# RWKV attention into a GELU layer: the pairs of zero products behind the first tile's bursts are left out

## The chip, the cores and the metric

One core of one Trainium2 chip runs the whole program. The time is the device's, in microseconds (us), from launch to end; the kernel before was run three times: 587.01, 589.43 and 590.76 us, median 589.43. Engines: TensorE (PE; its weight loads are listed apart as PEld), VectorE (DVE), ScalarE (ACT), GpSimd (POOL) and SyncE (SP), which issues most of the transfers.

## What is computed

For each of 4 batches and 8 heads (head size 48, 768 time steps) a state of 48 x 48 is carried through time. Its rows decay by `w`, and each step adds an outer product:

```
cur   = (u * k_t) outer v_t
y_t   = r_t @ (state + cur)
state = w_t[:, None] * state + k_t outer v_t
```

The y of all heads, laid side by side, are 3072 rows of 384 columns. They go through a layer: h = x @ w_in (384 x 2048), the exact GELU, and @ w_out (2048 x 384). All inputs are float32 or are turned into it in the kernel.

## The kernel before

The time axis is cut into tiles of 384 steps, two per batch: eight tiles, numbered x = 0 to 7. While the layer of tile x - 1 runs, the attention of a later tile is prepared beside it. The order of the work is written by hand: each tile has a string in `PLAN`, in which every letter takes one step of one generator ("." and "s" are the two units of tile 0, "f" the next tile's attention, "c" the conversion of the weights, "l" the loads, "x" larger groups of zero products). Engines then work through their own queues in that order and wait for one another by semaphores.

Inside a tile, steps are handled in chunks of 64. Within a chunk the matrix of decayed products r·k is built by halves: for each level h = 1, 2, 4, 8, 16, 32 (`LEVELS`, `halves()`), TensorE multiplies k by r for all chunks (a burst), the blocks of that level are copied out of PSUM into `a_sb`, and VectorE multiplies the decay over h steps into r and k, so that the next level can use them. So the next burst of a unit waits for that unit's update, and an update waits for the burst before it, which still reads r and k.

Tile 0 is special. It starts before any layer work is there, and its heads are split into two units that alternate, so that one unit's burst can run beside the other's update. Level 1 of a unit is done in `with_diagonal()` (L497); levels 2 to 32 in `products()` (burst at L478). Results go into pairs of PSUM banks from a pool of three (`pair`). Updates are at L557 (levels 2 to 16) and L546 (level 1, the k of level 32); copies into `a_sb` at L506, L508 and L570 on VectorE, and for levels 16 and 32 at L565 on ScalarE. After the levels come the transposes of k (L744, copied out at L746), the products k·v (L791) and a·v (L781), the chain of states on VectorE (L806), a fence (L822), the products of r with the state (L855), the copies to x transposed (L862, L878, L885), and then the layer's first product h (L1282). The weights arrive as 64-bit floats and are converted piece by piece on ScalarE (L356 to L359) and VectorE (L368, L372).

The kernel also issues products whose operands are zeros and whose result nobody reads (`keep_warm`, L248): each is a 128 x 128 load and a 512-wide bfloat16 product into a PSUM bank. 14 stand at the start, 7 behind the first unit's level 1 and 7 behind the products a·v of tile 0 (`warm()`), and in tile 0 two behind every burst of `products()`: 48 in all, 20 of them behind bursts. Those behind bursts use a single bank from `bank()`, which takes the two single banks in turn.

Of the kernel before, what the change touches and what calls it, by code (L numbers as in the profile page):

```python
# [91 lines left out]
def kernel(  # L92
# [31 lines left out]
    def pair(name):  # L124
        return pools["d"].tile([128, 2, BANK], F32, name=name, tag="d")
# [14 lines left out]
    def bank(name="o_ps"):  # L140
        turns[0] ^= 1
        return ps.tile([128, BANK], F32, name=name, tag=f"mm{turns[0]}")
# [99 lines left out]
    def keep_warm(n, elsewhere=False):  # L242
        if elsewhere:
            t = pair("warm")[:, 0]
        else:
            t = bank("warm")
        for _ in range(n):
            nc.tensor.matmul(t, lhsT=zeros[:, 0:128], rhs=zeros, start=True, stop=True)  # L248
# [127 lines left out]
    def attention(x, unit):  # L376
# [91 lines left out]
        else:  # L468
            yield

        def products(bs, right, width, rest=False):
            d = pair("d")
            n = 0
            for b in bs:
                for i in range(NI):
                    for g in range(2):
                        for p in range(2):
                            nc.tensor.matmul(d[half[p], g, n * width:(n + 1) * width],  # L478
                                             lhsT=kc[half[g], b, i, p], rhs=right(half[g], b, i, p),
                                             start=True, stop=True)  # L480
                    n += 1
            if x == 0 and not rest:
                keep_warm(2)
            return d[:, :, 0:n * width]

        def with_diagonal():
# [24 lines left out]
        def diagonal():  # L511
            return [products([b], lambda z, b, i, p: rucs[b][z, i, p], C) for b in range(np_)]
# [7 lines left out]
        def halves():  # L520

            for h in LEVELS:
                m = C // 2 // h
                if np_ < NPART and h == 1:
                    ds = with_diagonal()
                elif np_ < NPART:
                    d = products(range(np_), lambda z, b, i, p: rc[z, b, i, p], C)
                    d = d.rearrange("p g (n m two j) -> p g n m two j", two=2, j=h, m=m)[:, :, :, :, 1, :]
                else:
                    right = rc.rearrange("p b i c (m two j) -> p b i c m two j", two=2, j=h)[:, :, :, :, :, 1, :]  # L530
                    d = products(range(np_), lambda z, b, i, p: right[z, b, i, p], C // 2)
                    d = d.rearrange("p g (n m j) -> p g n m j", j=h, m=m)
# [1003 lines left out]
```

## Time and profile before

| | |
|---|---|
| median of three runs | 589.43 us |
| profiled execution | 587.12 us, span 585.3 us |
| TensorE busy | 567.1 us, 97% of the span |
| weight loads busy | 506.5 us, 87% |
| VectorE busy | 466.3 us, 80% |
| ScalarE busy | 307.4 us, 53% |
| zero products (L248) | 48, 14.5 us busy, 2.3 to 38.3 us |
| first product of the layer, h (L1282) | starts at 44.24 us |
| first product with w_out (L1371) | starts at 90.69 us |

The profile is one execution with every instruction's start and duration. A row of the timeline gives the start, the length, the engine, the line, what it writes and reads, the shape, and the number of instructions merged; in square brackets stands how long the engine was idle before, and which event ended that. A float32 product appears as two records (24 products of a burst are x48). The records of a product overlap, since products are pipelined: a single record's duration is longer than the time from one start to the next.

### The profile page before, as it was taken

How to read it: one execution, taken by the hardware profiler on the slowest of the kernel's cores; microseconds unless marked ns; L12 is line 12 of the kernel's file. 1: busy time of each engine (PE TensorE's matmuls, PEld its weight loads, DVE VectorE, ACT ScalarE, POOL GpSimd, SP SyncE). 2: the span in 40 equal slices, each digit the busy share in tenths (PEclk: the TensorE clock that was granted, in tenths of full speed). 3: DMA queues.
4: the chain of work that ended last, by engine and by line, in shares of the span. 5: the costliest groups of instructions: out<-in, count | busy, mean ns of one | idle time of the engine just before them, and what ended most of it. 6: DMA issues, size and time to landing. Idle time of an engine off the chain costs nothing.

```text
span 585.3 us, 17572 instructions
## 1 busy us (share of the span) xinstructions
PE 567.1 (97%) x7494; PEld 506.5 (87%) x7494; DVE 466.3 (80%) x914; ACT 307.4 (53%) x731; POOL 9.4 (2%) x29
## 2 busy tenths in 40 slices
PE   7799999999999999999998999999999999999997
PEld 3576666699998899999998899999999999999997
DVE  6889958999979998687978999577988999543523
ACT  2568997236363465545563457535654357425510
POOL 3200000000000000000000000000000000000000
PEclk9999999999999999999999999999999999999999
DMA  8449931111032311430124210430114100210000
GB/s 303 173 123 357 369 129 46 34 62 54 3 78 79 101 49 19 100 119 11 46 39 127 86 38 6 110 111 31 55 23 131 44 3 2 42 46 1 1 16 33
DMA packets 51006, 46.82 MB, mean 80 GB/s; under 512 B 31728, under 2 KB 36080, under 8 KB 50928
## 3 DMA queue, kind: packets, MB, share of 16 engines
q1 hardware_dynamic: 50160, 45.11, 24.9%
q8 instruction: 59, 0.97, 0.7%
q10 hardware_dynamic: 768, 0.59, 0.4%
q14 instruction: 19, 0.16, 0.1%
HBM read 36.24 MB, written 4.72 MB: 70 GB/s over the span
## 4 chain that ended last, share of the span: by engine, by line
PE 53%; DVE 5%; DMA 1%; issue 0%; ACT 0%; DVEq 0%; ACTq 0%
PE o_ps L1156 23%; PE u_ps L1032 16%; PE h_ps L1032 7%; PE d L654 3%; PE y_ps L781 1%; PE y_ps L855 1%; DMA out_dram<-o_sb 1%; PE kv_ps L791 1%; DVE e L1130 1%; DVE st L806 1%; DVE f L1130 1%; PE d L646 0%; DVE s L1130 0%; DVE tot_sb L437 0%; DVE o_sb L1130 0%
## 5 line engine op out<-in xcount | busy, mean ns | idle before, releaser
L1032 PE MATMUL u_ps<-x_home,w_in_sb 128*128 128x192 f32 x364 | 69.4, 329 | 0.5 <-DVE g L1069 0.4
L1032 PEld LDWEIGHTS u_ps<-x_home,w_in_sb 128*128 128x128 f32 x364 | 60.0, 190 | 2.3 <-DVE g L1069 1.1
L1156 PE MATMUL o_ps<-w_out_sb,g 128*128 128x192 f32 x224 | 41.0, 331 | 0.0
L1043 ACT ACTIVATE g<-g 128x384 f32<-128x384 f32 x66 | 32.5, 520 | 10.1 <-DVE g L1069 10.1
L1156 PEld LDWEIGHTS o_ps<-w_out_sb,g 128*128 128x128 f32 x224 | 36.4, 190 | 1.3
L670 ACT COPY a_sb<-d 32x256 f32<-32x256 f32 (+8 forms) x90 | 32.6, 363 | 8.5 <-PE d L654 7.0
L1072 ACT COPY g<-u_ps 128x384 f32<-128x384 f32 x56 | 26.6, 480 | 19.8 <-PE u_ps L1032 18.6
L1069 DVE TENSOR_TENSOR g<-g,h_ps 128x384 f32<-128x384 f32 x42 | 23.0, 548 | 14.8 <-PE h_ps L1032 14.8
L1282 PE MATMUL h_ps<-xT,w_in_sb 128*128 128x384 f32 x96 | 33.7, 497 | 0.7 <-ACT rkw L1287 0.6
L1165 ACT COPY o_sb<-o_ps 128x192 f32<-128x192 f32 x29 | 9.3, 319 | 47.2 <-PE o_ps L1156 38.0
L1156 PE MATMUL o_ps<-w_out_sb,f 128*128 128x192 f32 x176 | 30.9, 328 | 1.6 <-ACT o_sb L1165 1.6
L1156 PE MATMUL o_ps<-t,e 128*128 128x192 f32 x176 | 31.7, 331 | 0.0
L806 DVE SCALAR_TENSOR_TENSOR st<-st,tot,kv_ps 128x48 f32<-128x48 f32 x120 | 21.9, 258 | 12.2 <-PE kv_ps L791 12.2
L1156 PE MATMUL o_ps<-t,s 128*128 128x192 f32 x176 | 31.2, 330 | 0.0
L1156 PE MATMUL o_ps<-w_out_sb,e 128*128 128x192 f32 x176 | 30.9, 327 | 0.0
L1156 PEld LDWEIGHTS o_ps<-w_out_sb,f 128*128 128x128 f32 x176 | 28.8, 190 | 2.0 <-ACT o_sb L1165 1.9
L1156 PE MATMUL o_ps<-t,g 128*128 128x192 f32 x176 | 30.4, 326 | 0.0
L1156 PEld LDWEIGHTS o_ps<-t,e 128*128 128x128 f32 x176 | 28.6, 190 | 1.0 <-ACT o_ps L1172 0.3
L1032 PE MATMUL h_ps<-xT,w_in_sb 128*128 128x192 f32 x140 | 28.2, 332 | 1.1 <-issue 1.1
L1069 DVE TENSOR_TENSOR g<-g,u_ps 128x384 f32<-128x384 f32 x42 | 22.8, 550 | 7.8 <-PE u_ps L1032 7.5
L1156 PEld LDWEIGHTS o_ps<-w_out_sb,e 128*128 128x128 f32 x176 | 28.8, 190 | 0.1
L1156 PEld LDWEIGHTS o_ps<-t,s 128*128 128x128 f32 x176 | 28.6, 190 | 0.4
(215 smaller groups left out, 1266.2 us busy)
## 6 DMA issues: line engine op xcount, KB each, us to landing
rkw<-in_rkw_dram SPq DMA_DIRECT2D x54, 256.0 KB, 3.4
raw<-in_w_out_dram SPq DMA_DIRECT2D x8, 768.0 KB, 7.1
v_in<-in_v_dram SPq DMA_DIRECT2D x8, 584.0 KB, 4.6
raw<-in_w_in_dram SPq DMA_DIRECT2D x5, 768.0 KB, 6.6
out_dram<-o_sb SPq DMA_DIRECT2D x20, 192.0 KB, 2.0
kt_home<-x_home SPq DMA_DIRECT2D x72, 48.0 KB, 2.1
rkw<-in_rkw_dram SPq DMA_DIRECT2D x6, 384.0 KB, 5.9
raw<-in_w_in_dram SPq DMA_DIRECT2D x9, 256.0 KB, 5.3
```

Source lines behind the costliest of these rows:

```text
L654: nc.tensor.matmul(o[half[p], i * 3 * C // 2:(i + 1) * 3 * C // 2], lhsT=kc[half[g], n // NI, n % NI, p], rhs=rx[half[g], 2 * n + p], star ...
L670: nc.scalar.copy(out=at[z, g, first:behind, (a + 1) * h:], in_=d[z, :, :, to] if g == slice(None) else d[z, :, to])
L781: nc.tensor.matmul(y[p][half[g ^ swap(b)], i * C:(i + 1) * C], lhsT=vs(b, i, g)[half[p]], rhs=at[half[p], g, b * NI + i, :], start=(i == 0 ...
L806: nc.vector.scalar_tensor_tensor(out=stq[:, q, c], in0=stq[:, q, c - 1] if c else b4[:, q, NC - 1], scalar=totq[:, q, c:c + 1], in1=kvs[q ...
L1032: nc.tensor.matmul(o, lhsT=lhsT, rhs=rhs, start=start, stop=True, skip_group_check=True)
L1043: nc.scalar.activation(out=o, in_=z, func=AF.Gelu, scale=scale)
L1069: nc.vector.tensor_add(o, *(a if len(a) > 1 else (o, a[0])))
L1072: nc.scalar.copy(out=o, in_=a)
L1130: steps.append(("a", lambda: f(*(a() for a in args))))
L1156: nc.tensor.matmul(t[name], lhsT=lhs(j), rhs=rhs(j), start=start and j == 0, stop=(j == HF - 1), skip_group_check=True)
L1165: return lambda: nc.scalar.copy(out=to(), in_=t[name])
L1282: nc.tensor.matmul(h_ps, lhsT=w_in_sb[:, f // FI, j, f % FI * 128:(f % FI + 1) * 128], rhs=xT[:, j, :], start=(j == 0), stop=(j == NJ - 1))
```

## The change

`products()` no longer issues two zero products behind its burst in tile 0; its argument `rest`, which no caller sets, goes with it. The 28 other zero products stay.

```
-        def products(bs, right, width, rest=False):
+        def products(bs, right, width):
             d = pair("d")
             n = 0
             for b in bs:
...
                     n += 1
-            if x == 0 and not rest:
-                keep_warm(2)
             return d[:, :, 0:n * width]
```

More of the change, by code (lines that the diff above doesn't have):

```diff
@@ L469, in attention, with products @@
             yield
-        def products(bs, right, width, rest=False):
+        def products(bs, right, width):
             d = pair("d")
@@ L481, in products @@
                     n += 1
-            if x == 0 and not rest:
-                keep_warm(2)
             return d[:, :, 0:n * width]
```

## The prediction

> **What bounds the kernel now.** I read the page's busy shares and chain first, then the waits, then the timelines of TensorE (PE), VectorE (DVE) and ScalarE (ACT) from 8 to 48 us, where the removed products stand.
>
> ```profile
> PE 567.1 (97%) x7494; PEld 506.5 (87%) x7494; DVE 466.3 (80%) x914; ACT 307.4 (53%) x731; POOL 9.4 (2%) x29
> ...
> PE 53%; DVE 5%; DMA 1%; issue 0%; ACT 0%; DVEq 0%; ACTq 0%
> ...
> 50.00:55.00 5.00, 5.00 (x108) 3.35 (x107) 4.90 (x9) 4.97 (x9) 0.00 (x0) 1.00 1.05 392
> 55.00:60.00 5.00, 5.00 (x108) 3.35 (x107) 5.00 (x6) 4.81 (x7) 0.00 (x0) 1.00 1.05 398
> ```
>
> PE is the bound overall; from 44 us on it has hardly a gap (two lines of the table by stretch are shown: span, PE, PE loads, DVE, ACT busy, then clock and DMA). So a microsecond by which that dense part starts earlier is a microsecond at the end, if nothing between takes it back. The removed products lie earlier, between 12.7 and 31.8 us. PE's rows there (start, duration, what):
>
> ```profile
> 12.67 0.61 PE L248 MATMUL warm<-zeros 128*128 128x512 bf16 x2
> 14.02 0.93 PE L478 MATMUL d<-rkw 64*64 64x64 f32 x48 [0.74 <-DVE rkw L557]
> 14.88 0.60 PE L248 MATMUL warm<-zeros 128*128 128x512 bf16 x2
> 15.41 1.54 PE L497 MATMUL d<-rkw 64*64 64x128 f32 x48
> ...
> 18.99 0.61 PE L248 MATMUL warm<-zeros 128*128 128x512 bf16 x2
> 19.64 0.93 PE L478 MATMUL d<-rkw 64*64 64x64 f32 x48
> ...
> 24.72 0.93 PE L478 MATMUL d<-rkw 64*64 64x64 f32 x48 [1.05 <-DVE rkw L557]
> 25.58 0.60 PE L248 MATMUL warm<-zeros 128*128 128x512 bf16 x2
> 26.11 0.93 PE L478 MATMUL d<-rkw 64*64 64x64 f32 x48
> ```
>
> And DVE's rows that had to wait for such a burst:
>
> ```profile
> 20.63 1.84 DVE L557 TENSOR_TENSOR rkw<-rkw,tot_sb 128x768 f32<-128x768 f32 x2 [0.22 <-PE d L478]
> ...
> 28.51 0.96 DVE L557 TENSOR_TENSOR rkw<-rkw,tot_sb 128x768 f32<-128x768 f32 x1 [0.44 <-PE d L478]
> ...
> 29.91 0.56 DVE L546 TENSOR_TENSOR rkw<-rkw,tot_sb 128x384 f32<-128x384 f32 x1 [0.41 <-PE d L478]
> 31.30 0.56 DVE L546 TENSOR_TENSOR rkw<-rkw,tot_sb 128x384 f32<-128x384 f32 x1 [0.84 <-PE d L478]
> ```
>
> To see: up to 25 us PE waits for DVE (idle 0.74 and 1.05 us before bursts), and most pairs of zeros fill such idle time. From 25.6 to 31.6 it turns: burst, zeros, burst, zeros without a gap, and DVE waits.
>
> **The change, part by part.** It removes ten pairs of zero products (20 loads, 20 products) and adds nothing. The instruction lists agree otherwise, on every engine. Ten turns of the two single PSUM banks go too; ten is even, so later users get the same bank. A pair costs PE 0.53 us: 25.58 to 26.11. All ten: 5.3 us. What counts is what they hold up. I call the units A and B with their level, in PE's order: A2, A4, B1, A8, B2, B4, B8, A16, B16, A32, B32.
>
> 1. Behind A2 (12.67): nothing. A4 waits for DVE until 14.02.
> 2. Behind A4 (14.88): B1 can start at 14.90 instead of 15.41 and end at 16.44. DVE's update after B1 started at 17.11, B1's end (16.95) plus 0.16; DVE was free at 16.47. So it starts at 16.60: 0.51 earlier. (The profile calls that 0.64 us of DVE idle "issue", but it ends with the burst.)
> 3. Behind A8 (18.99): A8 stands still until 18.14 after four of its products, marked "issue"; I leave that moment where it is, so A8 ends at 19.0. B2 then follows at once, ends near 19.9, and DVE's update at 20.63 can start at 20.0 (DVE is free at 19.9): 0.6 earlier in all.
> 4. Behind B2 and B4 (20.50, 23.07): nothing of their own; B4 and B8 wait for DVE, which is busy 4.78 of the 5 us from 20 to 25. The 0.6 stays.
> 5. Behind B8 (25.58): A16 runs at 25.0 to 25.9, but DVE reaches A16's update only at 27.45, after B8's masked copy: still about 0.6.
> 6. Behind A16 (26.98): B16 starts at 26.1 after B8's update, ends at 27.0. DVE, free at 27.45, updates it then instead of 28.51: 1.06 earlier.
> 7. Behind B16: A32 needs A16's update (27.45): 27.5 to 28.4, its update 28.5 instead of 29.91: 1.4.
> 8. Behind A32: B32 at 28.45 to 29.4, its update 29.45 instead of 31.30: 1.85.
> 9. Behind B32 (31.17): the transposes, 31.61 before, can run at 29.55. They need PSUM that ACT's ten copies (L565, 27.16 to 30.86) release, and these start when B8's masked copy ends, 0.6 earlier. The copies end at 30.25, so ACT's copy of the first transpose, 32.46 before, starts at 30.35: 2.1.
>
> What is late next is thus ACT's row of copies, not DVE or PE. Behind it stands a chain without slack: k·v products (33.31), ten state updates a unit (34.66 and 36.70), the fence (38.46), the products with the state (38.66), x transposed, h at 44.24; each waits for the one before, so 2.1 passes on. I take **2.0**, of ends 0 and 2.1 while the clock holds. 0 would be a fixed time behind: from 48 to 75 us ACT is nearly full too (4.97 and 4.81 of 5) and the DMA share is 1.05. I choose near 2.1 because the weights' transfers that fill that stretch are issued from 43.21 on, behind this same chain, and move with it; and the last piece of w_in is converted at 66 to 67 us and first read at 84.21.
>
> Against the profiled execution, 587.12 us (span 585.3): 585.1. That execution was 2.3 below the median of 589.43; against the median, **587.4**.
>
> **The clock: the other half of the change.** The page prints a granted clock of 1.0 everywhere, but the records of the zeros themselves show two speeds:
>
> ```profile
> L248 PE MATMUL warm<-zeros x8: 608/634/634, 2.3 to 5.2; 128*128 128x512 bf16 x8
> ...
> L248 PE MATMUL warm<-zeros x4: 379/379/379, 6.3 to 6.9; 128*128 128x512 bf16 x4
> ```
>
> (The first row is of the window up to 5.6 us, the second of 6.5 to 8.) Eight products start in 2.9 us, 0.41 each; later seven take 1.68, so (1.68 - 0.38) / 6 = 0.22 each. PE starts at about half speed and is at full speed after some 3.8 us of work. It then never falls back, with idle gaps of up to 1.27 us (before 8.60) and with PE busy for 2.13 to 2.66 us of each 3.4 from 6.1 to 26.5. Without the zeros there would be a stretch, 19.9 to 24.1 us, with only one burst of 0.93 us and gaps of 1.1 and 1.5 to 2.1. No row of before shows whether 22% busy holds the clock.
>
> [...]
>
> What half speed costs, from these rows: a burst of 0.93 takes (0.93 - 0.22) x 1.9 + 0.42, about 1.8, so 0.87 more.
>
> **Rivals.**
> - *The clock falls in the sparse stretch, near 23 us, and returns within a window or two of the dense run from 24 us.* B8 and A16, maybe B16, run 0.87 longer each; DVE's update after B8 is 1.0 later than in my sum, later ones 1 to 3. Net from 1 us faster to 2 slower: 588.4 to 591.5, say 589.6.
> - *Slower: the clock falls there and stays down until the dense part.* Deciding point: whether bursts of 64-wide products, 0.93 us each, count as enough work. The updates end 1.7 later than before; transposes +0.6, k·v and y of both units about +2.0, the seven zeros left at 36.56 outlast DVE's states by 2.3. That is +6.6 if those seven raise the clock again, as the first fourteen did; if not, state products +2.0, x = 1's products +3.2 and the start of h +1: about +13. 596 to 602, say 599.5. For it: the pairs are the only products of 128x128 from 16.9 to 31.6 us. Against: a burst is dense too (48 records of 218 ns lie within 0.93 us), and no record of a burst in before is slow.
> - *Given back:* the 2 us are lost between 45 and 90 us to ACT or the weights' DMA, or by a changed instruction fetch (one "issue" stall there is 1.09 us). 589.4. For it: ACT waits 0.61 for a piece of w_in at 49.94. Against: the working of the 2.0.
> - That nothing is removed is excluded by the instruction lists. A gain over 5.3 us would need more than all the zeros' time.
>
> **How the numbers follow.** Forecast 0.48; short fall 0.17; long fall 0.20; given back 0.11; other, faster 0.04. 1% (5.9 us) is about what a measurement of this kernel can tell from no change. Faster by over 1%: 0.04; slower by over 1%: the long fall and a bad short one, 0.22; within: 0.74. The likeliest case alone lies at 585.5 to 589.4. The range takes in the milder part of the long fall, up to 598, and leaves out the rest of it and most of the fast end: 585 to 598.
>
> **What would show it.** Right: A16 to B32 back to back with DVE, h's first product near 42.2 us instead of 44.24, 64x64 records still at 218 ns, PE's busy time 5 us less. The clock step is wrong if 64x64 records between 20 and 36 us show a longer median or the seven zeros at about 35 us show 634 ns; the pass-on is wrong if h starts 2 us earlier but the first product with w_out, 90.69, does not.

## The result, and the profile after

The kernel after took a median of 594.17 us (591.22 to 597.87, ten runs); the kernel before, in ten runs beside it, 587.55 us (586.92 to 591.43). The ratio is 1.010, with a 95% interval of 1.0075 to 1.0125: the change costs about 6 us where a gain of 2 was forecast. A second set of runs (e10 below) gave 594.79 against 588.47, ratio 1.0112 [1.0069, 1.0155].

| | before | after |
|---|---|---|
| profiled execution, us | 587.12 | 593.89 |
| mean granted clock | 1.000 | 0.988 |
| TensorE busy, us | 567.1 | 566.4 |
| weight loads busy, us | 506.5 | 510.2 |
| zero products | 48 | 28 |
| update behind B32 starts | 31.30 | 31.93 |
| first product h starts | 44.24 | 49.58 |
| first product with w_out starts | 90.69 | 96.20 |
| from first h to TensorE's last product, us | 538.16 | 539.60 |

The page of after: busy shares, the granted clock in 40 slices of 14.8 us, a DMA queue, and the chain that ended last.

```profile
PE 566.4 (96%) x7471; PEld 510.2 (86%) x7474; DVE 466.3 (79%) x914; ACT 307.1 (52%) x731; POOL 7.9 (1%) x29
...
PEclk9689999999999999999999999999999999999999
...
q8 instruction: 59, 0.97, 0.7%
...
PE 46%; DVE 7%; DMA 2%; ACT 1%; SPq 1%; issue 1%; DVEq 0%; ACTq 0%
```

Twenty products and twenty loads are gone, but TensorE's busy time fell by only 0.7 us instead of 5, because what is left ran slower: the clock digits are 6 and 8 in the second and third slice. DVE's share of the chain rose from 5 to 7%. TensorE's rows in after:

```profile
14.38 0.93 PE L478 MATMUL d<-rkw 64*64 64x64 f32 x48 [1.28 <-DVE rkw L555]
...
16.96 0.34 PE L478 MATMUL d<-rkw 64*64 64x64 f32 x8 [0.34 <-DVE a_sb L568]
19.06 2.62 PE L478 MATMUL d<-rkw 64*64 64x64 f32 x88 [1.75 <-issue]
22.75 1.59 PE L478 MATMUL d<-rkw 64*64 64x64 f32 x48 [1.07 <-DVE rkw L555]
25.81 4.90 PE L478 MATMUL d<-rkw 64*64 64x64 f32 x192 [1.48 <-DVE rkw L555]
30.94 0.93 PE L478 MATMUL d<-rkw 64*64 64x64 f32 x48 [0.23 <-DVE raw L227]
...
35.23 0.60 PE L789 MATMUL kv_ps<-v_in,rkw 64*64 64x48 f32 x25
39.49 0.74 PE L789 MATMUL kv_ps<-v_in,rkw 64*64 64x48 f32 x20 [3.65 <-issue]
...
40.07 1.57 PE L779 MATMUL y_ps<-a_sb,v_in 64*64 64x64 f32 x47
...
49.58 0.59 PE L1280 MATMUL h_ps<-xT,w_in_sb 128*128 128x384 f32 x1
```

Two things stand there that before did not have. The bursts from 19.06 to 30 us are slow: B4 takes 1.59 us where an undisturbed burst takes 0.93 (the row at 30.94). And TensorE stops for 3.65 us in the middle of B's products k·v, marked "issue": the profile shows no engine and no data that it waits for. In before these products run through, and h follows at 44.24:

```profile
34.98 0.92 PE L791 MATMUL kv_ps<-v_in,rkw 64*64 64x48 f32 x48
...
44.24 2.24 PE L1282 MATMUL h_ps<-xT,w_in_sb 128*128 128x384 f32 x5
```

VectorE's rows of after in the same time:

```profile
21.73 1.83 DVE L555 TENSOR_TENSOR rkw<-rkw,tot_sb 128x768 f32<-128x768 f32 x2 [1.69 <-PE d L478]
...
27.44 0.96 DVE L555 TENSOR_TENSOR rkw<-rkw,tot_sb 128x768 f32<-128x768 f32 x1 [1.20 <-PE d L478]
...
31.93 0.56 DVE L544 TENSOR_TENSOR rkw<-rkw,tot_sb 128x384 f32<-128x384 f32 x1 [0.59 <-PE d L478]
...
40.38 0.26 DVE L809 COPY st<-kv_ps 128x96 f32<-128x96 f32 x1 [3.48 <-PE kv_ps L789]
```

VectorE still waits for bursts (1.69, 1.20, 0.59), only now for slow ones, and stands still with TensorE before 40.38.

The profiled difference of 6.77 us splits along the path: +0.63 up to the update behind B32 (0.35 of it is a later arrival of the first data: unit A's level 1 starts at 8.95 instead of 8.60); +4.71 from there to h (17.65 against 12.94), which is the stop of 3.65 and 1.06 more; +1.44 from h to the end. Up to the update behind B32 the falling clock, which the forecast watched, a little more than ate what the removal gained. The stop, which it did not expect, made most of the loss.

**The clock.** The record of the granted clock of after is 0.5 from 19.11 to 29.35 and from 39.59 to 43.00 us, else 1.0 over the span from its first entry, 5.46 us, on; it changes only at multiples of 3.413 us from one another and from that entry (6.06 us in before, where it stays at 1.0). By these windows (span, TensorE's busy time and records, granted clock, DMA share, GB/s), after and then before:

```profile
12.28:15.70 3.42, 2.14 (x120) 1.00 1.03 384
15.70:19.11 3.41, 1.32 (x48) 1.00 1.04 392
19.11:22.52 3.41, 2.57 (x88) 0.50 0.65 233
22.52:25.94 3.42, 1.71 (x52) 0.50 0.04 14
25.94:29.35 3.41, 3.41 (x128) 0.50 0.00 0
...
36.18:39.59 3.41, 0.10 (x6) 1.00 0.24 91
39.59:43.00 3.41, 3.19 (x74) 0.50 0.02 5
```

```profile
12.87:16.29 3.42, 2.68 (x84) 1.00 1.04 388
16.29:19.70 3.41, 2.28 (x80) 1.00 1.05 395
19.70:23.11 3.41, 2.54 (x99) 1.00 0.40 142
23.11:26.53 3.42, 2.37 (x83) 1.00 0.02 5
```

In these rows a window with 1.32 or 0.10 us of work at full clock is followed by half clock; one with 2.1 or more is not. At half clock, 2.57 us does not bring the clock back; 3.19 us and a full window do. The longest gap in the first window that lost the clock, 15.70 to 19.11, was 1.75 us; in these rows what goes with the loss is how little work the whole window holds, though not by a sharp border (last section).

**The stop.** The trace of after has 14,945 products and loads of TensorE and 150 waiting instructions between them, 15,095 in all, and one queue marked "instruction" (q8) carries 59 transfers of 16 KB: 255.9 instructions to a transfer (in before 15,138 and 59, 256.6). In the eighteen traces of this case, the stops of over 0.5 us marked "issue" in TensorE's rows between 17 and 49 us lie at its instructions number 448, 704, 1216, 1472, 1728, 1984 and 2240, waits counted in (a few records are missing, which moves the count by up to 12). These numbers differ by multiples of 256, and the stops end 2.1 to 2.9 us after such a transfer starts; two of these transfers never start less than 3.3 us apart (3.33 in before, 3.45 in after). From these numbers I take, as an estimate, blocks of 256 instructions, each asked for when TensorE passes the boundary a block earlier, but not sooner than some 3.4 us behind the one before. In after the block needed for k·v meets four transfers of w_in (1.5 MB), issued by SP just ahead; after, then before:

```profile
30.85 1.28 SPq L228 DMA_DIRECT2D raw<-in_w_in_dram  x3
32.18 0.42 SPq L223 DMA_DIRECT2D raw<-in_w_in_dram  x1
```

```profile
29.52 1.28 SPq L228 DMA_DIRECT2D raw<-in_w_in_dram  x3
30.85 0.43 SPq L223 DMA_DIRECT2D raw<-in_w_in_dram  x1
```

From the traces' records (us; "asked for" is worked out by this reading, the rest are records):

```
kernel   four issues     passes 1216   asked for   transfer starts   reaches 1472   stop
before   29.52 to 30.85     30.84        31.16         32.56            35.05       none
after    30.85 to 32.18     32.92        32.92         37.17            39.49       3.65
```

In before the block is asked for 0.31 us behind the fourth issue, the one of 768 KB, waits 1.4 us and is there just in time. In after the issues are 1.33 later, because a small fill on VectorE that releases the first of them (L227) comes behind the slow bursts. The passing is 2.08 later, because 40 fewer instructions lie ahead, so that boundary 1216 has also moved from burst B32 into the transposes. The block is asked for 0.74 us behind the fourth issue and waits 4.25 us. The experiments test this reading.

### The profile page after: what moved, and what is told of

Same layout as the page of the kernel before. It is cut to its first block, busy times and chain, and to the rows that moved or that the text cites. A ratio compares the mean times of both kernels' runs of the same rounds, so it can differ in the third digit from the quotient of the medians.

```text
span 592.1 us, 17529 instructions
## 1 busy us (share of the span) xinstructions
PE 566.4 (96%) x7471; PEld 510.2 (86%) x7474; DVE 466.3 (79%) x914; ACT 307.1 (52%) x731; POOL 7.9 (1%) x29
## 4 chain that ended last, share of the span: by engine, by line
PE 46%; DVE 7%; DMA 2%; ACT 1%; SPq 1%; issue 1%; DVEq 0%; ACTq 0%
PE o_ps L1154 19%; PE u_ps L1030 15%; PE h_ps L1030 7%; PE d L652 2%; SPq L583 1%; PE y_ps L853 1%; PE y_ps L779 1%; PE kv_ps L789 1%; ACT a_sb L668 1%; DVE g L1067 1%; DMA out_dram<-o_sb 1%; DMA kt_home<-x_home 1%; DVE e L1128 1%; DVE st L804 1%; DVE f L1128 0%
## 5 line engine op out<-in xcount | busy, mean ns | idle before, releaser
L1070 ACT COPY g<-u_ps 128x384 f32<-128x384 f32 x56 | 26.6, 480 | 19.9 <-PE u_ps L1030 18.8
L478 PEld LDWEIGHTS d<-rkw 64*64 64x64 f32 x1056 | 20.2, 156 | 10.6 <-DVE rkw L555 4.5
L1154 PEld LDWEIGHTS o_ps<-t,g 128*128 128x128 f32 x176 | 28.9, 190 | 0.0
```

Source lines behind the costliest of these rows:

```text
L478: nc.tensor.matmul(d[half[p], g, n * width:(n + 1) * width], lhsT=kc[half[g], b, i, p], rhs=right(half[g], b, i, p), start=True, stop=True)
L1070: nc.scalar.copy(out=o, in_=a)
L1154: nc.tensor.matmul(t[name], lhsT=lhs(j), rhs=rhs(j), start=start and j == 0, stop=(j == HF - 1), skip_group_check=True)
```

## The experiments

All medians in us, against the kernel before on the same chip. The profile of a run is one of its executions, and executions of one kernel differ by several us (586.74 to 593.52 for before beside e1 to e4), so a row read below is that execution's.

| run | median | before there | ratio [95%] |
|---|---|---|---|
| e1 ten pairs 64 wide | 590.42 | 588.05 | 1.0028 [1.0002, 1.0055] |
| e2 after, weights issued earlier | 590.45 | 588.05 | 1.0027 [1.0005, 1.0048] |
| e3 last five pairs 64 wide | 592.56 | 588.05 | 1.0064 [1.0037, 1.0091] |
| e4 before, weights issued earlier | 589.62 | 588.05 | 1.0016 [0.9988, 1.0044] |
| e5 before, weights issued near 20 us | 590.88 | 589.56 | 1.0003 [0.9969, 1.0037] |
| e6 after, weights issued near 20 us | 592.13 | 589.56 | 1.0039 [1.0004, 1.0075] |
| e7 e5 without the last five pairs | 593.33 | 589.56 | 1.0045 [1.0011, 1.0079] |
| e8 before, 18 zeros at the start | 590.65 | 589.56 | 1.0017 [0.9979, 1.0056] |
| e9 after, 20 narrow zeros at the start | 591.42 | 588.47 | 1.0046 [1.0021, 1.0071] |
| e10 after, again | 594.79 | 588.47 | 1.0112 [1.0069, 1.0155] |
| e11 before, four zeros behind B2, B4 | 589.13 | 588.47 | 1.0001 [0.9970, 1.0031] |
| e12 after, 20 narrow zeros near 36 us | 592.50 | 587.96 | 1.0071 [1.0041, 1.0102] |
| e13 before, the same 20 | 593.74 | 587.96 | 1.0093 [1.0064, 1.0123] |
| e14 before, again (one run) | 591.76 | 587.96 | |
| e15 after, weights issued later | 590.50 | 588.97 | 1.0020 [1.0001, 1.0040] |
| e16 before, weights issued later | 589.67 | 588.97 | 1.0002 [0.9977, 1.0027] |

### e1: the pairs stay, 64 columns wide

```
-            if x == 0 and not rest:
-                keep_warm(2)
+            if x == 0:
+                keep_warm(2, width=BANK if ('AB'[unit], h) in [] else 64)
```

> All ten pairs of zero products become 64 columns wide instead of 512: the same number of PE instructions in the same places as in the kernel before, but hardly any work. Theory 1 (two separate causes: the clock falls without the zeros, and, apart from it, PE's instruction stream is 40 instructions shorter, so that the standstill of 3.65 us in the products k.v, a late block of instructions, comes about): clock at half speed somewhere in 19 to 30 us, no standstill over 1 us in k.v, first h at 44 to 45.5 us instead of 49.58, total 0 to 1.5 us over before. Theory 2 (the half clock alone does it, and the standstill is its consequence): standstill of over 3 us stays, total 5 to 8 us over before. My forecast's own mechanism (the zeros only cost time): 2 us under before.

The list is empty, so all ten pairs are 64 wide. This keeps the number of instructions but takes most of the zeros' work away. It lost 2.4 us, not 6. TensorE's rows, and its windows:

```profile
24.66 1.56 PE L478 MATMUL d<-rkw 64*64 64x64 f32 x48 [1.15 <-DVE rkw L557]
...
44.75 5.58 PE L1282 MATMUL h_ps<-xT,w_in_sb 128*128 128x384 f32 x15
```

```profile
20.29:23.71 3.42, 1.71 (x68) 1.00 0.17 61
23.71:27.12 3.41, 2.46 (x78) 0.50 0.02 5
27.12:30.54 3.42, 3.42 (x112) 0.50 0.02 5
```

The clock fell here too (bursts of 1.56 us), yet h starts at 44.75, half a microsecond later than before (0.32 of it a later arrival of the first data), and there is no stop in k·v. So the slow bursts alone do not make the 6 us. And 1.71 us of work in a window, half of it, was too little here. This execution took 588.04 us, 2.4 under the median of its ten; what the slower ones lost is not shown.

### e2 and e4: the weights issued some 6 us earlier

The three loads ("l") and the one queued behind them move ahead of eleven steps of the units; e2 on after, e4 on before:

```
-  "...s.cssss.ss.ss.lllsl..ss.l.ssc..."
+  "...s.clllssss.ss.ss.sl..ss.l.ssc..."
```

> The changed kernel, with three loads of w_in (and the one queued behind them) issued some 6 us earlier, while the DMA queues are idle (21 to 30 us), so that no large transfer is queued when PE asks for its next blocks at 31 to 36 us. Theory 1: clock at half speed in 19 to 29 us as in the changed kernel, but no standstill in k.v; first h at 44 to 45.5 us, total 0 to 1.5 us over before. Theory 2: standstill stays, total 5 to 8 us over before.

> The kernel before with the same earlier loads as e2. Theory 1 (before had no late block of instructions to speak of): within 0.7 us of before, so that what e2 gains over the changed kernel is the standstill and not the loads as such. Rival (the earlier loads help in themselves): 2 us or more under before.

In e2 the issues lie at 23.40 to 24.74; the stop in k·v is 0.74 us and h starts at 45.63. But TensorE is now idle for 1.62 us up to 33.22, at boundary 1216, 2.36 us after a block's transfer (30.86): by the reading above the queue has only met another block, though the profile puts this wait down to VectorE. The clock was at half from 25.17 to 28.59. The loss fell from 6 to 2.4 us. On before the move gains nothing clear of the noise (e4).

### e5 and e6: the weights issued near 20 us

```
-  "...ssssscs.s.cssss.ss.ss.lllsl..ss..."
+  "...ssssscllls.s.cssss.ss.ss.sl..ss..."
```

> The kernel before with the four transfers of w_in issued at about 20 us instead of 29.5, so that they are over by 26 us. It is the partner of e6. Theory 1 (clock and block wait are two causes): the clock as before (no half window or one, 3.4 us each), no standstill over 1 us in k.v, total within 1 us of before. Rival (these loads matter by themselves): more than 1.5 us off.

> The changed kernel with the same four transfers issued at about 20 us. Theory 1: two to four half windows as in the changed kernel, at some 1.5 to 2 us each beyond the first 2 us that the missing zeros save; no standstill over 1 us in k.v after 31 us; total 1 to 3 us over before, so 3 to 5 under the changed kernel. Rival (the standstill comes from the half clock): standstill of over 3 us stays, 5 to 7 us over before.

With the weights out of the way in both, leaving the zeros out costs 592.13 - 590.88 = 1.25 us; the two intervals overlap. TensorE's rows in e6:

```profile
36.64 0.50 PE L789 MATMUL kv_ps<-v_in,rkw 64*64 64x48 f32 x20 [1.01 <-issue]
...
46.00 4.46 PE L1280 MATMUL h_ps<-xT,w_in_sb 128*128 128x384 f32 x13
```

h starts 0.87 earlier than in e5 (46.87): part of the forecast's gain is there against e5, but both are later than before (44.24). From h to the end, e6 takes 541.6 against 538.38.

### e3 and e7: only the last five pairs

In e3 the pairs behind B8, A16, B16, A32 and B32 are 64 wide, the others full:

```
+                keep_warm(2, width=BANK if ('AB'[unit], h) in [('A', 2), ('A', 4), ('A', 8), ('B', 2), ('B', 4)] else 64)
```

> Full pairs behind A2, A4, A8, B2 and B4, pairs of 64 columns behind B8, A16, B16, A32 and B32: steps 5 to 9 of the prediction by themselves, with the clock held through the sparse stretch and the instruction count of before. Theory 1 and the prediction's steps 5 to 9: clock at full speed throughout, h starts 1.0 to 1.6 us earlier than before, total 1 to 2 us under before. Rival (the last five pairs are needed for the clock, or ACT or the weights' DMA give the time back): within 0.5 us of before or over it.

A miss: +4.5 us instead of a gain. The profile has a stop of 3.21 us in k·v and half clock from 26.98 to 30.39 and from 40.63 to 44.05; the windows ahead of these hold 1.25 and 0.26 us of work. The first of these windows, 23.57 to 26.98, ends before B8's burst (27.08), so none of the five narrow pairs lies in it: this fall is not theirs. The kernel before, with all pairs full, loses the clock in the same stretch ahead of B8 in e4's profile (1.40 us of work from 23.98 to 27.39). The second follows the stop, and the block was asked for 0.38 us behind the fourth issue. So this run does not test steps 5 to 9 with the clock held.

e7 leaves the same five pairs out, with the weights issued as in e5:

```
-            if x == 0 and not rest:
+            if x == 0 and ('AB'[unit], h) in [('A', 2), ('A', 4), ('A', 8), ('B', 2), ('B', 4)]:
```

> Pairs of zeros behind A2, A4, A8, B2 and B4 only, those behind B8 to B32 left out, and the four transfers issued at about 20 us: the prediction's steps 5 to 9 without the clock's fall in the sparse stretch and without the block wait behind the weights. If those steps hold: h up to 1.5 us earlier than in before, total 0.5 to 1.5 us under e5. Rival (PE can't use the time, because its blocks of 256 instructions come no faster than one in 3.45 us): h within 0.5 us of e5's, idle times of PE that end 2.3 to 2.5 us after a block's transfer starts in its place.

Another miss. Its profile has h at 45.62, 1.25 earlier than e5, and 0.96 earlier if both are measured from the first data (8.93 against 9.22): under half of the 2.1 that steps 6 to 9 of the forecast name. The median is still 2.45 us above e5: every one of its ten runs had a mean clock of 0.997 or less, where half of e5's had 1.0. That speaks for these pairs holding the clock in some runs, but the profile doesn't show it: its slow window, too, follows one (21.40 to 24.81) that ends before B8's burst (25.05).

### e8 and e11: more zeros

`keep_warm(18)` instead of 14 at the start (e8); four zeros instead of two behind B2 and B4 (e11):

```
+                keep_warm(4 if unit and h in (2, 4) else 2)
```

> The kernel before with 18 zero products at the start instead of 14 (0.87 us more, in PE's idle time before the first burst). In runs of before the mean granted clock shows either no half window or one; the runs with none lie near 587.4, those with one near 589.2. If the fall comes from the idle time before a late first burst: no half window in most runs, total 0.4 to 1 us under before. Rival (it comes from elsewhere): as before, within 0.3 us.

> The kernel before with four zero products instead of two behind B2 and B4, where PE waits 0.5 and 1.05 us for DVE anyway. Half of before's runs show one half window, and those are some 2 us longer. If the sparse stretch (20 to 25 us) causes them: fewer runs with a half window, 0.5 to 1.5 us under before. Rival (they come from the wait for the first data): share of runs with a half window as in before, within 0.5 us.

Neither gains. e8 still had a slow window, 25.91 to 29.33. e11 raised the least work in any 3.41 us between 9 and 31 us from 1.69 us (before) to 2.13, and 6 of its ten runs had a mean clock of 1.0, against 9 of 19 for before: too small a difference to tell.

### e9 and e12: the instructions put back elsewhere

20 narrow zeros (40 instructions) are added to after, behind the first 14 (e9) or behind the seven near 36 us (e12), so that the instructions behind tile 0's bursts have the number again that they have in before (in e9 the bursts themselves come up to 40 numbers later).

```
     keep_warm(14)
+    keep_warm(10, width=64)
+    keep_warm(10, width=64)
```

```
-        for _ in range(2):
-            keep_warm(7, True)
+        for narrow in (0, 20):
+            keep_warm(7, True, narrow)
```

> The changed kernel with 20 zero products of 64 columns right behind the first 14, in PE's idle time before the first data: 40 instructions more, so that from there on every instruction of PE has its number of before, while nothing stands behind the bursts. Theory 1 (the instruction number at which PE asks for its next block, against the weights' transfers, makes the standstill): clock at half speed in one or two windows between 19 and 30 us, no standstill over 1.2 us in k.v, 1.5 to 3.5 us over before, and the stretch from the first h to the end 538 to 538.6 us as in before instead of 539.6. Rival (the bursts without zeros run too fast for the blocks, wherever these are cut): standstill of over 3 us stays, 5 to 7 us over before.

> The changed kernel with 20 zero products of 64 columns behind the last group of seven (some 36 us): tile 0's bursts stay as changed, but from there on every instruction of PE has its number of before. Theory (where the blocks of 256 instructions are cut in the rest of the kernel costs 1 to 2 us): standstill in k.v and half windows as in the changed kernel, but 538 to 538.6 us from the first h to the end instead of 539.6 to 541.2; total 3.5 to 5 us over before. Rival (the rest is longer for another reason, or by chance): 539.5 us or more from h, total 6 us over before.

e9 was to lose the stop, and kept it: 3.27 us. The boundary was back in its place, but the block's transfer still waited 5.16 us: TensorE passed 1216 at 32.58, ahead of the fourth issue (33.12), but the block before had started only 2.6 us earlier, and by the reading above the request came 0.23 behind that issue. So the place of the boundary is not all; when the block is asked for, against the transfers ahead, matters too. Both kernels show something else: from h to the end they take 537.45 and 538.28, as before does (538.16), not 539.60 or 541.18 (after, e10). e12's row of the stop:

```profile
37.85 0.50 PE L791 MATMUL kv_ps<-v_in,rkw 64*64 64x48 f32 x20 [2.95 <-issue]
```

### e13: the same 20 zeros in before

> The kernel before with the same 20 narrow zero products in the same place, 40 instructions more from there on. If any other cut of the blocks is worse: 539 us or more from h to the end, 1 to 2 us over before. If only the changed kernel's is: 537.9 to 538.6, within 0.7 us of before.

The edit is that of e12. From h to the end it takes 540.95, like after: in these profiles shifting the numbers by 40 the other way costs as much as shifting them back saves. Over the profiles in which the instructions from h on keep their numbers (or move by 8), the mean is 538.3 us (eleven profiles, 537.45 to 539.39); where they move by 20 or 40, 540.4 (seven, 539.37 to 541.60). The two groups touch, and other things differ between their kernels, so that the numbering makes the 2 us is likely, not shown. e13 also lost 4 us ahead of h, 1.75 of it in a new stop:

```profile
47.94 0.34 PE L480 MATMUL d<-rkw,rkw 64*64 64x64 f32 x7 [1.75 <-issue]
```

### e10 and e14: both kernels again, unchanged

> The changed kernel as it is, beside e9 on the same chip. Theory 1: 5 to 7 us over before, mean granted clock of 0.994 or less in nearly every run, a standstill of over 3 us in the products k.v.

> The kernel before, for a second profile. From h to the end 538.2 us as in the first, if that is steady; the block asked for at instruction 1216 starts either about 3 us behind the first of the weights' transfers (no standstill) or about 6 (standstill of 3 us): both can be, since the first profile lies close to the border.

e10 confirms after: a stop of 3.38 us, half clock from 19.32 to 29.56 and 39.80 to 43.21. e14 surprised me. Before itself can have the stop; TensorE's rows, and its windows:

```profile
39.10 1.03 PE L791 MATMUL kv_ps<-v_in,rkw 64*64 64x48 f32 x42 [2.90 <-issue]
...
49.28 0.91 PE L1282 MATMUL h_ps<-xT,w_in_sb 128*128 128x384 f32 x2
```

```profile
22.54:25.95 3.41, 1.79 (x70) 1.00 0.04 12
36.19:39.60 3.41, 0.51 (x35) 1.00 0.15 55
39.60:43.02 3.42, 3.42 (x75) 0.50 0.02 5
```

The stop brings h to 49.28, nearly as late as in after, with all zeros in place and the clock at 1.0 until 39.6. It also brings the slow window behind it: 0.51 us of work in the window with the stop. And a window with 1.79 us held the clock. Here TensorE passed 1216 at 31.73, as the fourth issue began (31.75), but the block before had started only 2.45 us earlier (29.28), and the transfer started at 36.64.

Over all runs with the four issues in one row, the moment at which the block is asked for, counted from the fourth issue, sorts the short waits from the long ones, but for e9:

```
run      asked for, us behind the fourth issue   transfer starts, us later
e1                -0.39                                1.7
e8                -0.01                                1.3
e11                0.08                                2.0
e13                0.23                                1.8
before             0.31                                1.4
e9                 0.23                                4.4
e3                 0.38                                4.0
after              0.74                                4.2
e10                0.74                                4.0
e14                0.93                                4.0
e12                0.95                                3.4
```

The border lies between about 0.2 and 0.4 us, no sharper than the asking time is worked out (e9, 0.23, waits long, and before, 0.31, does not), and before lies on it; the change pushes the kernel over it. Which of the transfers ahead the block waits for is not resolved further.

### e15 and e16: the weights issued later

The second to fourth transfer of w_in go behind the updates of A32 and B32; e15 on after, e16 on before:

```
-  "...ss.ss.lllsl..ss.l.ssc...lsss..."
+  "...ss.ss.sl..sslll.l.ssc...lsss..."
```

> The kernel after, with the issue of the second, third and fourth transfer of w_in (256, 256 and 768 KB) put in the program behind the updates of A32 and B32 instead of ahead of them; nothing else is changed. Theory 'the block of instructions waits behind those transfers': the transfer that carries the block with the products k·v is then asked for ahead of them, so PE's standstill there (3.65 us after) is under 1.0, h starts at 45 to 47 us instead of 49.6, and the time is 2 to 3.5 us over before: 0.6 to 1.3 of slower clock and about 2 of the stretch behind h. Rival 'the standstill comes from the slower clock or from where the blocks end alone': it stays, and the time is 5 to 7 us over before.

> The kernel before with the same three transfers put behind the updates of A32 and B32. Theory 'the block waits behind those transfers, and before lies just at the edge of it': the edge is further away, so the standstill that one execution of before had (2.90 us) cannot come, and the time is 0 to 1 us under before. Rival 'the weights are then converted later and the layer waits for them': ScalarE and VectorE convert later, the time is 1 to 3 us over before.

TensorE's rows in e15, then its windows:

```profile
24.93 5.09 PE L478 MATMUL d<-rkw 64*64 64x64 f32 x192 [1.49 <-DVE rkw L555]
30.30 0.93 PE L478 MATMUL d<-rkw 64*64 64x64 f32 x48 [0.28 <-DVE raw L227]
...
36.77 0.50 PE L789 MATMUL kv_ps<-v_in,rkw 64*64 64x48 f32 x20 [1.58 <-issue]
...
45.26 3.17 PE L1280 MATMUL h_ps<-xT,w_in_sb 128*128 128x384 f32 x9
```

```profile
19.14:22.55 3.41, 1.60 (x87) 1.00 0.64 237
22.55:25.96 3.41, 1.66 (x58) 0.50 0.02 5
25.96:29.37 3.41, 3.41 (x132) 0.50 0.02 5
```

All that moved is three transfers, with the small fills on VectorE that release them, and the loss fell from 6.3 (e10) to 1.5 us. The clock falls as in after, but the block waits 2.26 instead of 4.25 us, the stop shrinks from 3.65 to 1.58 (under 1.0 was expected), no slow window follows, and h starts at 45.26. The rival, that the slow clock or the block boundaries alone make the stop, falls. e16 gains nothing: stops of 0.70 and 0.81 us at later boundaries take the place, and h starts at 45.90. None of these kernels beats before.

## Why the prediction was wrong, point by point

- **Steps 1 to 3** held up to 17 us. A4 waits 1.28 for VectorE; the update behind B1 starts at 16.77 instead of 17.11, 0.69 earlier measured from the first data (0.51 forecast). Step 3 failed where it said of A8's standstill, marked "issue", "I leave that moment where it is": it ends at 19.06 instead of 18.14, since by the reading above it too is the wait for a block of instructions (number 448), and with 1.75 us it left its window 1.32 us of work. (Step 5 says that VectorE reaches A16's update at 27.45; by the rows of before, 28.07 less 0.6, that is where this update ends, and the later steps use it so.)
- **Steps 4 to 8** were lost in the clock. That the clock holds, as the 2.0 supposes, no row of before showed, nor how soon it would return from a fall; in after it stayed at half for three windows of 3.413 us. The forecast weighed "whether 22% busy holds the clock" in a stretch from 19.9 to 24.1; the clock went earlier, at 19.11, behind a window that was still 39% busy (1.32 of 3.41 us). Its reading that TensorE in before is busy for "2.13 to 2.66 us of each 3.4" held for one phase of the windows only: from 21.12 to 24.53 before has 1.69 us of work. A slow burst took 1.59 us, 0.66 more than a full one, where 0.87 was priced. The update behind B32 came at 31.93, not 29.45. The short fall (0.17), by which the clock "returns within a window or two of the dense run", describes this part: "net from 1 us faster to 2 slower" it said, and up to B32 it is 0.28 slower without the first data's delay (31.93 - 31.30 - 0.35).
- **Step 9 and the pass-on of 2.0** failed. The chain "without slack" behind B32 did not merely pass its start on; it got 4.71 us longer. The step's list of what each link waits for had engines and data in it, not TensorE's own instructions. The forecast had named such a stop once, in "a changed instruction fetch (one "issue" stall there is 1.09 us)", but only for 45 to 90 us, and priced at the loss of the gain, where a stop costs 3.65 us and the slow window behind it about 1.
- **"The instruction lists agree otherwise"** was true of the lists and wrong of their effect: 40 fewer instructions move each later boundary of 256 (by the reading above; 1216 from burst B32 into the transposes), and that belongs among what a change moves. The stretch behind h is 1.44 us longer in the profile (3.0 in e10), which the two groups of e13 lay to the shift without showing it. Which waits of the dense part make it is open: TensorE's idle time behind h, in gaps of over 0.15 us, rises only from 6.62 to 7.32 us, and the rest is spread over 500 us.
- **The deciding point of the long fall** ("whether bursts of 64-wide products, 0.93 us each, count as enough work") came out for the forecast: a full window of them, 3.41 us, does bring the clock back, and the fall ended at 29.35. The loss of its size came by the stop.
- **The tests named at the end** did their work: 64x64 records from 19 to 36 us have a median of 311 ns instead of 218, and h starts later, not earlier. Of the gain itself something under half was seen: with the weights issued near 20 us, h starts 0.87 (e6) and 0.96 us (e7, from the first data) earlier than in the same kernel with all zeros (e5), in one profile each.

In sum, of some 6.3 us: about 4.8 go with the block's wait behind the weights (6.3 in e10, of four runs on one chip, less 1.5 in e15 on another; by the intervals of the two, good to some 3 us), and the rest is what the slow clock and the longer stretch behind h cost beyond the gain.

## What to carry to other kernels

Before removing filler work, add up TensorE's work in every stretch of 3.41 us, the step of the clock's record here, at any phase: the clock was lost behind windows with up to 1.71 us of work (e1), and in after with no single gap over 1.75 us in the first of them. Treat "issue" stops as a queue of their own: count the engine's instructions to the next boundary (here 256 apart), and see what large transfers are issued around the moment the next block is asked for. A kernel can lie at the border of such a race without its profile showing a stop: the first profile of before has none in k·v, the second (e14) one of 2.90 us.

## What the runs showed of the hardware that was not expected

- Over the eighteen traces up to 54 us, the clock fell after every window of 3.41 us at full clock that held 1.41 us of TensorE's work or less, and held after every one with 1.79 or more. Between lies no sharp border: of fourteen such windows eight lost the clock (1.53 to 1.71 us; 1.60 in e15, 1.71 in e1) and six held it (1.51 in e6 from 18.05, 1.57 in after from 5.46, 1.64 in e9 from 16.21). So busy time alone does not settle it there. At half clock it did not return after 2.57 us of work or less, and did after 2.69 (e4 from 27.39) or more. In before the least busy 3.41 us between 9 and 31 us hold 1.69 us of work, so by the figures above the phase of the windows may decide whether the clock falls, which no run varied by itself: of 114 runs of before beside the experiments, 62 have a mean clock of 0.997 or less. On the chip of e1 to e4 the price can be read off: 15 runs of before with a mean clock of 1.0 average 587.52 us, 14 with 0.997 average 589.75, 2.2 us for one slow window and whatever came with it: some of these runs may hold a stop, as e14 does (0.996).
- TensorE's stops marked "issue", those over 0.5 us between 17 and 49 us, lie multiples of 256 instructions apart (numbers 448 to 2240), and end 2.1 to 2.9 us after a 16 KB transfer of the instruction queue starts. With 1.5 MB of weights issued ahead, the transfer starts 1.3 to 2.0 us after it is asked for, as worked out above, or 3.4 to 4.4; runs 0.23 us behind the fourth issue or earlier have the short wait but for e9, and those from 0.38 on the long one, with before (0.31) between.
- Three transfers issued two of VectorE's updates later (e15) were worth some 4.8 us to the kernel after (e10 less e15), though in the trace of after no wait between 28 and 50 us ends with the landing of a transfer.
